# Attention and two gated layers on one core: TensorE's attention work grouped by kinds in half-unit steps

## The chip, the cores and the metric

The kernel is one program on one core of a Trainium2 chip. A core has five engines with queues of their own, each in order: TensorE (PE, with its weight loads shown apart as PEld), VectorE (DVE), ScalarE (ACT), GpSimd (POOL) and SyncE (SP, which here only starts transfers). They wait for one another by semaphores. Operands lie in SBUF, products of TensorE in the eight banks of PSUM. The metric is the time of one execution on the device in microseconds (us). The kernel before takes 571.85 us, the median of three runs (571.66 to 571.90).

## The reference

All in float32: causal attention (2 batches, 12 heads, 448 positions, 64 features a head), its output laid out as 896 tokens by 768 features, then two layers on those tokens.

```python
scores = scale * np.matmul(q, k.transpose(0, 1, 3, 2))      # (2, 12, 448, 448)
scores = np.where(mask, -1000000000.0, scores)              # causal
attn = np.exp(scores - np.max(scores, axis=-1, keepdims=True))
attn = attn / (np.sum(attn, axis=-1, keepdims=True) + 1e-09)
x = np.matmul(attn, v).transpose(0, 2, 1, 3).reshape(896, 768)
x = (x @ w_a) * (x @ w_b) @ w_out                           # 768 -> 1536 -> 768
h = x @ w_in                                                # 768 -> 2048
out = (h * (1.0 / (1.0 + np.exp(-h)))) @ w_out2             # 2048 -> 768
```

## The kernel before

**The layers.** Products are taken as three passes: an operand is split into a rounded half `hi` and a remainder `lo` (type float32r), and hi·hi + hi·lo + lo·hi is summed in a PSUM bank (`mm`, L295). ScalarE makes `hi` by a copy, VectorE makes `lo` by a subtraction. Weights arrive as raw words and go through conversion steps on ScalarE (L213, L219, L252) and VectorE (L225, L230, L256), laid out by `Timeline.convert` over a stretch of the program. A stretch is measured in matmuls that have been written so far; in the attention part a slot counts as seven (`SLOT_MM`). The weights of the first granule (a pair of weight tiles) are converted over slots 8 to 34, those of the second over slots 35 to 52. Later granules use products of sums of blocks, for which sums of the input chunks are needed (`sums_of`, in steps from slot 44).

**Attention.** A unit is two heads of one batch, 12 units in all, the first six of batch 0. Its 448 queries are seven chunks `j` of 64; chunk `j` sees keys 0 to 64(j+1). The chunks go in four groups, `GROUPS = ((6,), (5, 0), (4, 1), (3, 2))`, one group a slot, four slots a unit. The stages of one group are these.

- `scores` (TensorE): chunks with j of 3 or more by the three passes in float32r, 128 keys by 128 queries to an array of 128x128 (L565); chunks 0 to 2, and all of unit 0, in plain float32 on half the columns of the array (L569, 128x64).
- `soft`: VectorE scales, masks and takes the minimum of the negated scores (L577), ScalarE takes the exponential and its sum (L581).
- `normalize`: VectorE forms the reciprocals of the sums for two groups at once (L590, L591), GpSimd multiplies the seven pieces `p` by them (L594).
- `transposes` (TensorE, float32, 128x128, L610): four 128x128 blocks a slot, written to one PSUM bank. They are copied to `ptr` in SBUF one slot later (L710), that of chunk 4 by VectorE, the six others by ScalarE.
- `pv` (TensorE, float32, 128x64, L627): the product with the values, `xo`, over four blocks of keys in three slots.
- `finish` / `arrive`: when `xo` is whole, ScalarE copies it twice, to `xh` (rounded, L383) and to `xf` (as it is, L385); VectorE makes `xl` (L389).

The halves of the next unit's `q` and `k` are made by GpSimd (`halves_hi`, L538) in a unit's first slot and VectorE (`halves_lo`, L543) in its third. The order on the engines is the order in which the program is written: in slot `s` stand the scores of group `s`, the `pv` of group `s-11`, the transposes of group `s-5`, and then what was put off to that slot, sorted by a priority (0 `finish`, 1 copies of transposes, 2 `soft`), then reciprocals, sums and conversions. PSUM banks: three for scores, two for transposes (`ps_t`; while batch 0 is unfinished a third), two for `xo`. From slot 50 on, TensorE also does products of the first layer that need batch 0 only (`early_products`).

**The end.** Each output block is copied from PSUM by ScalarE and sent by SP's queue (L920, L921). The very last one is cut in two: ScalarE copies and sends one half, VectorE and SP's queue the other (L914 to L917).

The order is set by these lines (L22 to L28 and L699):

```python
PV = ((0,), (1,), (2, 3), ())
EVAC_DVE = (4,)
LAG_N = 1
LAG_T = 5
LAG_PV = 11
ORDER = (("scores", 0), ("pv", LAG_PV), ("transposes", LAG_T))
...
for what, lag in ORDER:
    u, i = divmod(s - lag, NS)
```

Of the kernel before, what the change touches and what calls it, by code (L numbers as in the profile page):

```python
# [18 lines left out]
P = 128  # L19
D = 64  # L20
GROUPS = ((6,), (5, 0), (4, 1), (3, 2))
PV = ((0,), (1,), (2, 3), ())  # L22
COL = {j: c for c, j in enumerate(j for g in GROUPS for j in g)}
EVAC_DVE = (4,)
LAG_N = 1
LAG_T = 5
LAG_PV = 11
ORDER = (("scores", 0), ("pv", LAG_PV), ("transposes", LAG_T))  # L28
# [6 lines left out]
SLOT_HI = 0  # L35
SLOT_LO = 2
# [26 lines left out]
def fused_kernel(ctx: ExitStack, tc: tile.TileContext, qk, v, w_ab, w_mid, w_in, w_out, out):  # L63
# [327 lines left out]
    def sums_of(c):  # L391


        a11, a12, a21, a22 = (XF.pop((2 * c + i, b)) for b in range(B) for i in range(2))
# [11 lines left out]
        s3 = add("S", a11, a21, ALU.subtract)  # L406
        yield 2
# [69 lines left out]
    with tc.manual_schedule():  # L477

        with ExitStack() as actx:
# [33 lines left out]
            U = [dict() for _ in range(NU)]  # L513
            late, now = {}, [0]
            n_slots = NU * len(GROUPS) + LAG_PV + 2
            NS = len(GROUPS)
# [4 lines left out]
            def load_qk(u):  # L521
# [5 lines left out]
                nc.sync.dma_start(out=t["k"], in_=qk[u, :, 1, :])  # L527
# [22 lines left out]
            def scores(u, i):  # L550

                t = U[u]
                if i == 0:
                    for n in ("sums", "nmax", "rcp"):
                        t[n] = st_p.tile([P, NJ], F32, tag=n, name=n)
                bank = ps_s.tile([P, 512], F32, tag="s", name="sc")
                sm = sm_p.tile([P, S], F32, tag="sm", name="sm")
                o = 0
                for j in GROUPS[i]:
                    K = D * (j + 1)  # L560
                    sc = bank[:, o:o + K]
                    o += K
                    if "qh" in t and j >= BIG:
                        for n, (a, k) in enumerate((("qh", "kh"), ("qh", "kl"), ("ql", "kh"))):
                            nc.tensor.matmul(out=sc, lhsT=t[a][:, j - BIG].rearrange("p h q -> p (h q)"), rhs=t[k][:, 0:K],  # L565
                                             start=(n == 0), stop=(n == 2))
# [6 lines left out]
                    defer(0, 2, partial(soft, u, j, sc, sm[:, o - K:o], K, COL[j]))  # L573
# [25 lines left out]
            def transposes(u, i):  # L599
                t = U[u]  # L600
                if i == 0:
                    t["pt"] = pt_p.tile([P, NKB, 2, S], F32, tag="ptr", name="ptr")
                pool, tag = (ps_g[1], "g") if now[0] < b0_done - 4 and now[0] % 3 == 0 else (ps_t, "t")
                bank = pool.tile([P, NKB, 2, D], F32, tag=tag, name="pt")
                o = 0
                for j in GROUPS[i]:
                    pt = bank[:, o:o + nblk[j]]
                    o += nblk[j]
                    for kb in range(nblk[j]):
                        nc.tensor.transpose(  # L610
                            out=pt[:, kb].rearrange("p h q -> p (h q)"),
                            in_=p_sb[u % 2][j][:, kb * P:(kb + 1) * P], identity=ident,
                        )
                    copy = nc.vector.tensor_copy if j in EVAC_DVE else nc.scalar.copy
                    dst = t["pt"][:, 0:nblk[j], :, j * D:(j + 1) * D]
                    defer(1, 1, partial(copy, out=dst, in_=pt))

            def pv(u, kb):
# [12 lines left out]
                if kb == NKB - 1:  # L631
                    defer(1, 0, partial(finish, b, chunk, t["x"][:, 0:S]))
# [29 lines left out]
            line.now = -n_slots * SLOT_MM  # L662
            line.convert(granules[0], (CONV0 - n_slots) * SLOT_MM, (CONV1 - CONV0) * SLOT_MM)
            line.convert(granules[1], (CONV1 + 1 - n_slots) * SLOT_MM, (CONV2 - CONV1) * SLOT_MM)
# [11 lines left out]

            b0_done = (NP - 1) * NS + LAG_PV + NKB + 1
            fill, n_fill = early_products(), 2 * NP
            done_fill = 0
            fill0 = NU * NS + 2  # L680
            for s in range(n_slots):
                now[0] = s
                if s == NU * NS + 1:
# [5 lines left out]
                u, i = divmod(s, NS)  # L689
                if i == 0 and 0 < u and u + 2 < NU:  # L690
                    load_qk(u + 2)
                if i == SLOT_HI and u + 1 < NU:
                    halves_hi(u + 1)
                if i == SLOT_LO and u + 1 < NU:
                    halves_lo(u + 1)
                if i == 0 and 0 < u <= NU:
                    load_v(u - 1)
                for what, lag in ORDER:
                    u, i = divmod(s - lag, NS)  # L699
                    if not 0 <= u < NU:  # L700
                        continue
                    if what == "scores":
                        scores(u, i)
                    elif what == "transposes":
                        transposes(u, i)
                    else:
                        for kb in PV[i]:
                            pv(u, kb)
                for _, fn in sorted(late.pop(s, ()), key=lambda e: e[0]):
# [3 lines left out]
                u, i = divmod(s - LAG_N, NS)  # L713
                if 0 <= u < NU and i % 2 == 1:
                    normalize(u, (i - 1, i))
                if s >= SUMS0:
                    sums_x.step()
                line.to((s + 1 - n_slots) * SLOT_MM)
# [257 lines left out]
```

## Time and profile before

| | |
|---|---|
| median of 3 runs | 571.85 us |
| the profiled execution: its time, its span | 571.69 us, 569.9 us |
| TensorE busy | 559.3 us (98%), clock 0.999 |
| VectorE busy | 421.8 us (74%) |
| ScalarE busy | 380.5 us (67%) |
| GpSimd busy | 72.2 us (13%), all of it before 97 us |
| chain that ended last | PE 93%, DVE 2%, ACT 2%, POOL 1%, issue 1%, DMA 1% |
| last attention product on TensorE | ends at about 107.4 us |

The attention part is the first 107 us of the span, the two layers are the rest, in which TensorE has no gap. Times in the rows further down count from the start of the span. A row of a timeline gives the start, the duration and the instruction; durations of neighbours on one engine overlap, since an engine starts the next instruction before the last has drained, so what an instruction takes of its engine is read from one start to the next. "[1.00 <-ACT ptr L710]" at a row's end means that the engine had been idle for 1.00 us and that the instruction at L710 on ACT, which writes `ptr`, let it go on.

### The profile page before, as it was taken

How to read it: one execution, taken by the hardware profiler on the slowest of the kernel's cores; microseconds unless marked ns; L12 is line 12 of the kernel's file. 1: busy time of each engine (PE TensorE's matmuls, PEld its weight loads, DVE VectorE, ACT ScalarE, POOL GpSimd, SP SyncE). 2: the span in 40 equal slices, each digit the busy share in tenths (PEclk: the TensorE clock that was granted, in tenths of full speed). 3: DMA queues.
4: the chain of work that ended last, by engine and by line, in shares of the span. 5: the costliest groups of instructions: out<-in, count | busy, mean ns of one | idle time of the engine just before them, and what ended most of it. 6: DMA issues, size and time to landing. Idle time of an engine off the chain costs nothing.

```text
span 569.9 us, 8400 instructions
## 1 busy us (share of the span) xinstructions
PE 559.3 (98%) x2978; PEld 490.4 (86%) x2978; DVE 421.8 (74%) x794; ACT 380.5 (67%) x754; POOL 72.2 (13%) x127
## 2 busy tenths in 40 slices
PE   8999997999999999999999999999999999999997
PEld 6666664799999999999999999999999999999996
DVE  6798887587989898969875688978887798342500
ACT  4989988674766666668745475888786996532601
POOL 6887764000000000000000000000000000000000
PEclk9999999999999999999999999999999999999999
DMA  7355323032333434333333333333324233541501
GB/s 246 116 178 139 121 65 141 1 112 110 112 110 112 136 134 161 117 118 109 114 110 112 110 112 110 112 113 110 112 96 143 75 113 111 165 142 54 176 0 64
DMA packets 18233, 65.41 MB, mean 115 GB/s; under 512 B 2192, under 2 KB 6928, under 8 KB 18192
## 3 DMA queue, kind: packets, MB, share of 16 engines
q1 hardware_dynamic: 18048, 64.77, 33.6%
q8 instruction: 23, 0.38, 0.3%
q14 instruction: 18, 0.15, 0.1%
q10 hardware_dynamic: 144, 0.11, 0.1%
HBM read 62.13 MB, written 2.75 MB: 114 GB/s over the span
## 4 chain that ended last, share of the span: by engine, by line
PE 93%; DVE 2%; ACT 2%; POOL 1%; issue 1%; DMA 1%; SPq 0%; POOLq 0%; DVEq 0%; ACTq 0%
PE acc L295 82%; PE pt L610 4%; PE xo L627 3%; PE sc L565 3%; PE sc L569 2%; DVE sm L577 1%; POOL p L594 1%; ACT ptr L710 1%; DMA k<-qk 1%; DVE wq L230 0%; ACT xf L385 0%; ACT p L581 0%; ACT xh L383 0%; DVE kl L543 0%; DVE ql L543 0%
## 5 line engine op out<-in xcount | busy, mean ns | idle before, releaser
L225 DVE SCALAR_TENSOR_TENSOR wq<-wr 128x768 uint32<-128x768 uint32 (+1 forms) x76 | 66.5, 877 | 28.4 <-ACT wr L219 27.7
L318 ACT COPY s<-acc 128x448 f32<-128x448 f32 x72 | 38.4, 533 | 63.1 <-PE acc L295 62.7
L219 ACT ACTIVATE wr<-wr,wbias 128x768 uint32<-128x768 uint32 (+1 forms) x76 | 69.9, 920 | 0.0
L213 ACT ACTIVATE wr<-wr 128x768 f32<-128x768 f32 (+1 forms) x76 | 63.8, 840 | 5.4 <-DMA wr<-w_out 4.0
L230 DVE SCALAR_TENSOR_TENSOR wq<-wr,wq 128x768 uint32<-128x768 uint32 (+1 forms) x76 | 64.0, 873 | 0.1
L594 POOL TENSOR_SCALAR p<-p,rcp 128x448 f32<-128x448 f32 (+6 forms) x84 | 56.3, 685 | 21.3 <-ACT p L581 15.6
L581 ACT ACTIVATE p<-sm,nmax 128x448 f32<-128x448 f32 (+6 forms) x84 | 43.0, 523 | 10.5 <-DVE nmax L577 9.5
L295 PE MATMUL acc<-th,wgbl 128*128 128x448 f32 x168 | 49.5, 366 | 0.0
L295 PE MATMUL acc<-th,wgbh 128*128 128x448 f32 x168 | 49.4, 366 | 0.0
L295 PE MATMUL acc<-th,wgal 128*128 128x448 f32 x168 | 49.4, 365 | 0.0
L295 PE MATMUL acc<-tl,wgah 128*128 128x448 f32 x168 | 49.4, 366 | 0.0
L295 PE MATMUL acc<-tl,wgbh 128*128 128x448 f32 x168 | 49.4, 365 | 0.0
L295 PE MATMUL acc<-th,wgah 128*128 128x448 f32 x168 | 49.3, 365 | 0.0
L610 PEld LDWEIGHTS pt<-ident,p 128*128 128x128 f32 x192 | 20.2, 141 | 22.4 <-issue 10.8
L610 PE MATMUL pt<-ident,p 128*128 128x128 f32 x192 | 31.0, 285 | 5.5 <-ACT ptr L710 4.4
L577 DVE CUSTOM_DVE_ANT_0 sm<-sc,mask 128x448 f32<-128x448 f32 (+6 forms) x84 | 31.9, 411 | 4.8 <-PE sc L569 4.8
L295 PEld LDWEIGHTS acc<-th,wgbh 128*128 128x128 f32 x168 | 31.5, 188 | 2.9 <-DVE s L767 0.2
L295 PEld LDWEIGHTS acc<-th,wgah 128*128 128x128 f32 x168 | 31.5, 188 | 2.7
L295 PEld LDWEIGHTS acc<-tl,wgah 128*128 128x128 f32 x168 | 31.6, 188 | 2.6
L295 PEld LDWEIGHTS acc<-th,wgal 128*128 128x128 f32 x168 | 31.5, 188 | 2.5
L295 PEld LDWEIGHTS acc<-th,wgbl 128*128 128x128 f32 x168 | 31.5, 188 | 2.5
L295 PEld LDWEIGHTS acc<-tl,wgbh 128*128 128x128 f32 x168 | 31.5, 188 | 2.5
(167 smaller groups left out, 1384.2 us busy)
## 6 DMA issues: line engine op xcount, KB each, us to landing
wr<-w_ab SPq DMA_DIRECT2D x24, 768.0 KB, 4.9
wr<-w_in SPq DMA_DIRECT2D x16, 768.0 KB, 4.5
wr<-w_out SPq DMA_DIRECT2D x24, 512.0 KB, 4.4
wr<-w_mid SPq DMA_DIRECT2D x12, 768.0 KB, 4.6
v<-v SPq DMA_DIRECT2D x12, 256.0 KB, 4.2
q<-qk SPq DMA_DIRECT2D x24, 112.0 KB, 2.8
k<-qk SPq DMA_DIRECT2D x12, 224.0 KB, 3.3
out<-o SPq DMA_DIRECT2D x11, 224.0 KB, 5.4
```

The source lines that it names most:

```text
L213: nc.scalar.activation(out=word(i, 1).bitcast(F32), in_=word(i, 1).bitcast(F32), func=AF.Copy, scale=2.0 ** -112)
L219: nc.scalar.activation(out=word(i, 0), in_=word(i, 0), func=AF.Relu, bias=wbias, scale=2.0 ** -29)
L225: nc.vector.scalar_tensor_tensor(out=xi(i), in0=word(i, 1), scalar=3, in1=word(i, 0), op0=ALU.logical_shift_left, op1=ALU.bitwise_or)
L230: nc.vector.scalar_tensor_tensor(out=xi(i), in0=word(i, 1), scalar=0x80000000, in1=xi(i), op0=ALU.bitwise_and, op1=ALU.bitwise_or)
L295: nc.tensor.matmul(out=acc[:, 0:S], lhsT=w, rhs=a, start=first, stop=last, skip_group_check=True)
L318: nc.scalar.copy(out=t, in_=acc[:, 0:S])
L565: nc.tensor.matmul(out=sc, lhsT=t[a][:, j - BIG].rearrange("p h q -> p (h q)"), rhs=t[k][:, 0:K], start=(n == 0), stop=(n == 2))
L577: nc.vector.tensor_tensor_reduce(out=sm, in0=sc, in1=mask[:, S - K:S], op0=ALU.add, op1=ALU.min, scale=-(D ** -0.5), scalar=3.0e38, accum_ ...
L581: nc.scalar.activation(out=p_sb[u % 2][j][:, 0:K], in_=sm, func=AF.Exp, bias=t["nmax"][:, c:c + 1], scale=-1.0, accum_out=t["sums"][:, c:c ...
L594: nc.gpsimd.tensor_scalar(out=pj, in0=pj, scalar1=t["rcp"][:, COL[j]:COL[j] + 1], scalar2=1.0, op0=ALU.mult, op1=ALU.mult,)
L610: nc.tensor.transpose(out=pt[:, kb].rearrange("p h q -> p (h q)"), in_=p_sb[u % 2][j][:, kb * P:(kb + 1) * P], identity=ident,)
L627: nc.tensor.matmul(out=t["x"][h * D:(h + 1) * D, kb * P:S], lhsT=t["v"][:, kb, h * D:(h + 1) * D], rhs=t["pt"][:, kb, h, kb * P:S], start= ...
```

## The change

The slot becomes a step of two groups, two steps a unit, and in a step TensorE's work is ordered by kinds: first the float32r scores of both groups, then the plain ones, then `pv` (key blocks 0 and 1 in one step, 2 and 3 in the other), then all eight transposes. The lags become `LAG_T = 2` and `LAG_PV = 5` steps. The eight transposed blocks go to two banks and leave by seven copies in a new split (`COPIES`): in the first step one by ScalarE and three by VectorE, in the second three by ScalarE. ScalarE's copies have priority 0 now, `finish` 1, `halves_lo` and `soft` 2, VectorE's copies and `normalize` 3. A third bank is used in turn for units 0 to 7.

`arrive` makes no `xf` for batch 0; `sums_of` makes that chunk anew from `xh` and `xl` by an addition on VectorE (`whole`). The keys of unit 0 are sent for by ScalarE's queue instead of SP's. The early products are spread over four steps and stand first in a step. The last output block is no longer cut in two.

```diff
+COPIES = (
+    ((0, "scalar", 0, 2, 5, 2), (1, "vector", 2, 1, 5, 2), (1, "vector", 3, 1, 6, 1), (1, "vector", 0, 1, 0, 1)),
+    ((0, "scalar", 0, 1, 1, 4), (1, "scalar", 1, 1, 2, 3), (1, "scalar", 2, 1, 4, 1)),
+)
+LAG_T = 2
+LAG_PV = 5
+FILL_STEPS = 4
...
-        XF[chunk, b] = t = A.new(F32, "xf")
-        nc.scalar.copy(out=t, in_=src)
+        if b:
+            XF[chunk, b] = t = A.new(F32, "xf")
+            nc.scalar.copy(out=t, in_=src)
...
+    def whole(chunk):
+        hi, lo = XS[chunk, 0]
+        t = A.new(F32, "xf")
+        nc.vector.tensor_tensor(out=t, in0=hi[:].bitcast(F32), in1=lo[:].bitcast(F32), op=ALU.add)
+        return t
...
-                nc.sync.dma_start(out=t["k"], in_=qk[u, :, 1, :])
+                (nc.sync if u else nc.scalar).dma_start(out=t["k"], in_=qk[u, :, 1, :])
...
+                if groups[0] and u + 1 < NU:
+                    defer(0, 2, partial(halves_lo, u + 1))
+                for n in range(len(groups)):
+                    defer(0, 2, partial(soft_group, u, [(j, sc) for m, j, sc in work if m == n]))
...
+                for _ in range(2):
+                    pool, tag = (ps_g[1], "g") if n_banks[0] % 3 == 2 and u < NP + 2 else (ps_t, "t")
...
+                    if copy == "vector":
+                        defer(1, 3, partial(nc.vector.tensor_copy, out=dst, in_=src))
+                    else:
+                        defer(1, 0, partial(nc.scalar.copy, out=dst, in_=src))
...
+                while done_fill < min(n_fill * max(0, d + 1 - 2 * NU) // FILL_STEPS, n_fill):
+                    next(fill, None)
+                    done_fill += 1
+                if u < NU:
+                    scores(u, (2 * i, 2 * i + 1))
+                u, i = divmod(d - LAG_PV, 2)
+                if 0 <= u < NU:
+                    for kb in range(2 * i, min(2 * i + 2, NKB)):
+                        pv(u, kb)
+                u, i = divmod(d - LAG_T, 2)
+                if 0 <= u < NU:
+                    transposes(u, i)
+                u, i = divmod(d - 1, 2)
+                if 0 <= u < NU:
+                    defer(0, 3, partial(normalize, u, (2 * i, 2 * i + 1)))
...
-                if last and b == 1 and i == 1:
-                    o2, half = A.new(F32, "o2"), S // 2
...
+                nc.scalar.copy(out=o, in_=src)
+                nc.sync.dma_start(out=out[m + i, :, toks[b]], in_=o)
```

TensorE, first half of a unit in the middle of attention, before. `sc` are scores, `xo` the product with the values, `pt` the transposed pieces.

```order
L565 MATMUL sc<-kh,qh 128x448
L565 MATMUL sc<-kl,qh 128x448
L565 MATMUL sc<-kh,ql 128x448
L627 MATMUL xo<-ptr,v 64x320 x2
L610 MATMUL pt<-ident,p_3_124 128x128 x2
L610 MATMUL pt<-ident,p_2_123 128x128 x2
L565 MATMUL sc<-kh,qh 128x384
L565 MATMUL sc<-kl,qh 128x384
L565 MATMUL sc<-kh,ql 128x384
L569 MATMUL sc<-k,q_119 64x64 x2
L627 MATMUL xo<-ptr,v 64x192 x2
L627 MATMUL xo<-ptr,v 64x64 x2
```

The same half of a unit on TensorE after the change.

```order
L581 MATMUL sc<-kh,qh 128x448
L581 MATMUL sc<-kl,qh 128x448
L581 MATMUL sc<-kh,ql 128x448
L581 MATMUL sc<-kh,qh 128x384
L581 MATMUL sc<-kl,qh 128x384
L581 MATMUL sc<-kh,ql 128x384
L585 MATMUL sc<-k,q_119 64x64 x2
L667 MATMUL xo<-ptr,v 64x192 x2
L667 MATMUL xo<-ptr,v 64x64 x2
L655 MATMUL pt<-ident,p_6_134 128x2x64 x3
L655 MATMUL pt<-ident,p_6_134 128x128
L655 MATMUL pt<-ident,p_5_133 128x2x64 x3
```

The two groups of float32r scores stand in one piece, behind them everything on half the array, behind that seven of the half's eight transposes (the eighth is the next row).

ScalarE around the arrival of one unit of batch 0, before. `xo` is the finished product, `ptr` the transposed pieces in SBUF, `p` the exponentials.

```order
L383 CAST xh<-xo 128x448
L385 COPY xf<-xo 128x448
L710 COPY ptr<-pt 128x8x64
L581 ACTIVATE p_4_132,sums<-sm,nmax 128x320
L581 ACTIVATE p_1_129,sums<-sm,nmax 128x128
L710 COPY ptr<-pt 128x6x64
L710 COPY ptr<-pt 128x2x64
L581 ACTIVATE p_3_131,sums<-sm,nmax 128x256
L581 ACTIVATE p_2_130,sums<-sm,nmax 128x192
L710 COPY ptr<-pt 128x2x64
```

And after the change, over the same exponentials.

```order
L750 COPY ptr<-pt 128x4x128
L383 CAST xh<-xo 128x448
L608 ACTIVATE p_4_132,sums<-sm,nmax 128x320
L608 ACTIVATE p_1_129,sums<-sm,nmax 128x128
L608 ACTIVATE p_3_131,sums<-sm,nmax 128x256
L608 ACTIVATE p_2_130,sums<-sm,nmax 128x192
L750 COPY ptr<-pt 128x2x256
L750 COPY ptr<-pt 128x2x192
L750 COPY ptr<-pt 128x2x64
```

The copy of transposes stands ahead of `xh`, there is no `xf`, and the copies of a half stand together instead of one behind each group.

VectorE where the last unit's scores are worked on, after the change. `xf<-xh,xl` is the new addition of `whole`, `S` the sums.

```order
L617 TENSOR_SCALAR sums<-sums 128x4
L618 RECIPROCAL rcp<-sums 128x4
L396 TENSOR_TENSOR xf<-xh,xl 128x448
L408 TENSOR_TENSOR S<-xf 128x448
L604 ISA sm,nmax<-sc,mask 128x320
L604 ISA nmax 128x1
L604 ISA sm,nmax<-sc,mask 128x128
L604 ISA nmax 128x1
L604 ISA sm,nmax<-sc,mask 128x256
L604 ISA nmax 128x1
L604 ISA sm,nmax<-sc,mask 128x192
L604 ISA nmax 128x1
```

The addition stands ahead of the last unit's `sm`; the sums' first subtraction stood in the same part of the program before, with `xf` read as ScalarE had left it.

## Rows read from the trace of the kernel before

**Rows 1.** Windows: us, then busy us (instructions) of PE, PEld, DVE, ACT, POOL; clock; DMA

```profile
27.37:63.70 36.33, 36.33 (x282) 24.33 (x280) 33.06 (x120) 33.85 (x116) 30.29 (x47) 1.00 0.47 144
27.37:41.90 14.53, 14.53 (x114) 9.73 (x112) 14.12 (x49) 12.91 (x47) 12.44 (x18) 1.00 0.46 157
73.50:85.00 11.50, 11.23 (x88) 7.59 (x89) 11.36 (x38) 8.97 (x34) 9.33 (x12) 1.00 0.25 74
```

**Rows 2.** Waits from 19 to 108 us: total us, times, longest

```profile
PE pt L610 <- ACT ptr L710: 4.4, 6, 1.4
DVE xl L389 <- ACT xf L385: 9.6, 7, 2.4
```

**Rows 3.** Timeline of TensorE: start us, us, tile<-operands, shape, count, [idle before <-releaser]

```profile
57.12 0.66 PE L610 MATMUL pt<-ident,p 128*128 128x128 f32 x4
57.53 0.45 PE L565 MATMUL sc<-kh,qh 128*128 128x448 f32 x1
57.82 0.36 PE L565 MATMUL sc<-kl,qh 128*128 128x448 f32 x1
58.02 0.37 PE L565 MATMUL sc<-kh,ql 128*128 128x448 f32 x1
58.31 0.76 PE L627 MATMUL xo<-ptr,v 128*64 128x320 f32 x4
...
61.85 0.44 PE L569 MATMUL sc<-k,q 128*64 128x128 f32 x4
62.22 0.66 PE L610 MATMUL pt<-ident,p 128*128 128x128 f32 x4
```

**Rows 4.** Timeline of TensorE, two transposes that wait

```profile
73.48 0.63 PE L610 MATMUL pt<-ident,p 128*128 128x128 f32 x4 [1.00 <-ACT ptr L710]
...
89.95 0.63 PE L610 MATMUL pt<-ident,p 128*128 128x128 f32 x4 [1.39 <-ACT ptr L710]
```

**Rows 5.** Timeline of ScalarE around one arrival

```profile
63.70 0.55 ACT L385 COPY xf<-xo 128x448 f32<-128x448 f32 x1
64.13 0.61 ACT L710 COPY ptr<-pt 128x512 f32<-128x512 f32 x1
64.61 0.59 ACT L581 ACTIVATE p<-sm,nmax 128x320 f32<-128x320 f32 x1
```

**Rows 6.** Timeline of VectorE

```profile
57.71 0.93 DVE L256 TENSOR_TENSOR wgbl<-wq,wgbh 128x768 fp32r<-128x768 f32 x1
...
82.77 1.09 DVE L230 SCALAR_TENSOR_TENSOR wq<-wr,wq 128x768 uint32<-128x768 uint32 x1
83.78 0.55 DVE L710 COPY ptr<-pt 128x384 f32<-128x384 f32 x1
84.25 0.61 DVE L577 CUSTOM_DVE_ANT_0 sm<-sc,mask 128x448 f32<-128x448 f32 x1
...
85.08 0.59 DVE L398 TENSOR_TENSOR S<-xf 128x448 f32<-128x448 f32 x1
```

**Rows 7.** Timeline of GpSimd, the same three scalings twice

```profile
43.75 1.49 POOL L594 TENSOR_SCALAR p<-p,rcp 128x448 f32<-128x448 f32 x3 [0.83 <-ACT p L581]
...
57.96 2.04 POOL L594 TENSOR_SCALAR p<-p,rcp 128x448 f32<-128x448 f32 x3 [0.84 <-ACT p L581]
```

**Rows 8.** Timeline of TensorE, the first scores

```profile
5.17 3.52 PE L569 MATMUL sc<-k,q 128*64 128x448 f32 x28 [0.34 <-DMA k<-qk]
```

**Rows 9.** The last output: timeline; lines L920, L921 (ns, us); L917

```profile
566.52 0.34 ACT L914 COPY o<-acc 128x224 f32<-128x224 f32 x1 [1.92 <-PE acc L295]
...
566.90 0.39 DVE L915 COPY o<-acc 128x224 f32<-128x224 f32 x1 [20.18 <-ACT o L914]
...
L920 ACT COPY o<-acc x11: 532/534/546, 487.0 to 564.1; 128x448 f32<-128x448 f32 x11
...
DMA to landing us min/median/max: 1.9/5.4/6.2
...
DMA to landing us min/median/max: 1.7/1.7/1.7
```

More of the change, by code (lines that the diff above doesn't have):

```diff
@@ L389, in arrive @@
         return lambda: nc.vector.tensor_tensor(out=lo, in0=src, in1=hi[:].bitcast(F32), op=ALU.subtract)
+    def whole(chunk):
[3 more added lines that the diff above has]
+        return t
     def sums_of(c):
-        a11, a12, a21, a22 = (XF.pop((2 * c + i, b)) for b in range(B) for i in range(2))
+        a21, a22 = (XF.pop((2 * c + i, 1)) for i in range(2))
+        a11, a12 = whole(2 * c), None
+        yield 1
         def add(name, a, b, op):
@@ L406, in sums_of @@
         s3 = add("S", a11, a21, ALU.subtract)
+        yield 1
+        a12 = whole(2 * c + 1)
         yield 2
@@ L661, in fused_kernel @@
             load_ahead()
[L662 to L664 removed]
+            line.now = -2 * n_steps * SLOT_MM
+            line.convert(granules[0], (CONV0 - 2 * n_steps) * SLOT_MM, (CONV1 - CONV0) * SLOT_MM)
+            line.convert(granules[1], (CONV1 + 1 - 2 * n_steps) * SLOT_MM, (CONV2 - CONV1) * SLOT_MM)
             first = []
@@ L675, in early_products @@
                         yield
[L677 to L683, printed above, removed]
+            fill, n_fill, done_fill = early_products(), 2 * NP, 0
+            for d in range(n_steps):
+                now[0] = d
+                u, i = divmod(d, 2)
+                if u == NU and i == 0:
                     sctx.close()
@@ L688, in fused_kernel @@
                     banks.add(ctx.enter_context(right(name="ps_r", bufs=3, space=PSUM, reuse_waits="tile")), 3)
-                u, i = divmod(s, NS)
                 if i == 0 and 0 < u and u + 2 < NU:
                     load_qk(u + 2)
-                if i == SLOT_HI and u + 1 < NU:
+                if i == 0 and u + 1 < NU:
                     halves_hi(u + 1)
-                if i == SLOT_LO and u + 1 < NU:
-                    halves_lo(u + 1)
                 if i == 0 and 0 < u <= NU:
                     load_v(u - 1)
[L698 to L709, printed above, removed]
+                while done_fill < min(n_fill * max(0, d + 1 - 2 * NU) // FILL_STEPS, n_fill):
[13 more added lines that the diff above has]
+                    defer(0, 3, partial(normalize, u, (2 * i, 2 * i + 1)))
+                for _, fn in sorted(late.pop(d, ()), key=lambda e: e[0]):
                     fn()
@@ L712, in fused_kernel @@
                     tasks.pop(0)()
[L713 to L718, printed above, removed]
-                want = n_fill * max(0, s + 1 - fill0) // (n_slots - 3 - fill0)
-                while done_fill < min(want, n_fill):
-                    next(fill, None)
-                    done_fill += 1
+                for n in range(2):
+                    if 2 * d + n >= SUMS0:
+                        sums_x.step()
+                    line.to((2 * d + n + 1 - 2 * n_steps) * SLOT_MM)
             run(fill)
```

85 lines of the change are left out of this document (41 added, 44 removed).

## The prediction

> **What bounds the kernel now.** I read the page first: TensorE is busy for 98% of the span at full clock, and the chain that ended last is 93% TensorE. Of the layers the change touches only the last output. So I read the attention part by windows. Five units between two starts of `xo` for keys of block 0 take 36.33 us, 7.27 us each, and TensorE is busy for all of it [rows 1]. The others are not far behind: per unit ScalarE is busy 33.85/5 = 6.77, VectorE 6.61, GpSimd 6.06 us. In two of these units VectorE has 14.12 of 14.53 us, and from 73.50 to 85.00 us 11.36 of 11.50 [rows 1]. The reader is to see that TensorE sets the pace with little air behind it. Next I asked who lets TensorE go on: in the attention part it waits 4.4 us in six places, each time before transposes, until ScalarE has emptied a bank [rows 2, 4]. Last I read one unit on TensorE start by start, for what a change of kind costs.
>
> **TensorE's work by kinds.** The three float32r passes over 448 columns start at 57.53, 57.82 and 58.02, and the next kind at 58.31: 0.29, 0.20 and 0.29 us for equal work [rows 3]. The middle one has its own kind on both sides, so entering a group of this kind costs 0.09 and leaving it 0.09. A unit has four such groups before and two after: 4 x 0.09 = 0.36 saved. In all a unit goes from 14 changes of kind to 8. The other two that go are entries into transposes. 64-query scores with 128 columns take 0.37 from their start to the transposes [rows 3]; how much of it is the change no row shows alone. From below it is 0; from above 0.17, if such a change costs what entering and leaving a float32r group do together. I take 0.14, near the upper end, since four small matmuls lie in those 0.37. So 0.36 + 2 x 0.14 = 0.64 a unit (bounds 0.36 and 0.70): 6.63 in place of 7.27. From the first `xo` to the last scores nine units are done: 9 x 0.64 = 5.8 us (3.2 to 6.3). Behind the last scores the order has about nine changes fewer, at 0.1 each 0.9 us (0.4 to 1.4).
>
> One rule of the Trainium skill speaks against the full term. TensorEngine Tiling, section Key Properties, says that changing the tiling mode drains the engine, and that changing the tile within a mode doesn't. By it only the changes between 128x128 and 128x64 cost anything, eight a unit before and four after. The row agrees at 58.31, where 128x64 follows; it differs at 57.53, where the array stays 128x128 behind transposes and the first pass is still 0.09 slower [rows 3].
>
> **What waits for ScalarE.** For batch 0 `xf` goes: 0.43 us from start to start, in six units [rows 5]. Transposes leave by four copies in place of six, 1536 columns in place of 1664; at 0.48 us for 512 columns [rows 5] that is 0.12 a unit at least, and with two starts less I take 0.2. ScalarE's 6.77 becomes 6.14 a unit, inside the 6.63. The copies now stand ahead of `xh` instead of behind `xh` and `xf`, which is some 0.8 us of queue before the copy that TensorE waits for. Of the 4.4 us [rows 2] I let 2.4 go (bounds 0 and 4.4): the conversion steps in ScalarE's queue stay where they were, and with them part of waits as long as 1.00 and 1.39 [rows 4].
>
> **What VectorE gets.** Three copies of 512 columns in all in place of one of 384, which takes 0.47 from start to start [rows 6]: 128 columns more are 0.16, two more starts 0 to 0.3; I take 0.3 a unit. Where conversions fall (1.01 each from start to start [rows 6]) there is no room. The two units to 41.90 need 14.12 + 0.6 = 14.7 us of VectorE against 2 x 6.63 = 13.3 of TensorE: 1.5 over, of which I let 0.3 be absorbed, +1.2. From 73.50 to 85.00 us TensorE's 11.23 busy us [rows 1] are 1.54 units and become 10.2, VectorE's 11.36 becomes 11.8: +1.6. In those late units only two banks serve the transposes, and the second transposes of a unit wait for VectorE's copies, which stand behind `ql`, `kl` and four `sm`; three places at up to 0.6, mostly the same waits, +0.3. The early products come first in the step behind the last scores and write where scores were, so they wait for VectorE's last `sm`: 0 to 1.0, I take +0.3. New waits: +3.4 (bounds 0, if short queues hide them all, and 6.5).
>
> The six additions of `whole` take about 0.5 each, as the like subtraction `S` [rows 6]. Two stand near the last scores, four behind, where VectorE had air: it stood idle for `xf` up to 2.4 us at once, 9.6 in all [rows 2], and `xh` alone comes sooner. I cost them at nothing on the path; without that cover they cost 3.0. GpSimd's three scalings take 1.49 us beside copies from PSUM and 2.04 beside a conversion that reads two tiles of SBUF [rows 6, 7]. The Trainium skill, SBUF — State Buffer, section SBUF: two separate sides, gives the reason: such an instruction and GpSimd lock each other out of a shared port pair for its whole length. By that rule two additions ahead of the last scalings would hold TensorE up by up to 1.0 more, 566.7.
>
> **Start and end.** TensorE waits 0.34 us for the first keys [rows 8]. Sent for by a queue that is free, they land behind the warm-up products: -0.3 (0 to -0.34). What queues behind that issue on ScalarE is its table load, far ahead of its first exponential. SP's next loads start one issue earlier. At the end, before, VectorE's half starts at 566.90, only when ScalarE's is done; its 0.39 us and 1.7 to landing [rows 9] end at 569.0. After, one copy of 0.53 starts at 566.52 like ScalarE's half before, and its transfer takes at least 1.9 [rows 9]: 569.0 as well. I cost it at 0 (-0.3 to +0.5; the median of 5.4 was measured with weights in flight, of which none are left).
>
> **The sum.** -5.8 - 0.9 - 2.4 + 3.4 - 0.3 + 0 = -6.0 us. The profiled execution took 571.69 us (569.9 of span and 1.8 around it), 0.16 under the median of 571.85. 571.69 - 6.0 = 565.7 us. All bounds together give from -13 to +3 us.
>
> **The rivals.**
>
> *VectorE becomes the bound all through.* For: 6.61 + 0.3 = 6.91 a unit, above TensorE's 6.63, and two windows without air [rows 1]. Against: the 6.61 holds two of the most loaded units, and VectorE now finds `xh` ready, where it waited 9.6 us [rows 2]. At 97% use a unit takes 7.12: 9 x 0.15 = 1.3 gained, with 0.9 and 0.8 of the other terms 568.7.
>
> *Slower: the shorter way from sums to transposes.* Five slots, 9.1 us, become two steps, 6.6 us. In between stand VectorE's whole next step, with the reciprocals last in it, and three scalings of 1.5 to 2.0 [rows 7]. I count 0.5 to 1.0 us of air: VectorE's reciprocals 2.2 to 3.9 us into a step, the scalings, then the transposes 5.3 to 6.2 us after that step's start. A VectorE that lags by 2 us stalls every transpose of the step. It decides from 0.32 us of stall a step on, where the 0.64 a unit is used up; at 0.5 in 18 steps it costs 9 against 5.8 + 0.9 + 0.3 gained, with nothing else counted: 573.7. Against: a stalled TensorE has already given VectorE the step's scores, so the lag does not feed itself.
>
> *Only the drain counts* (the rule of the Trainium skill above). Four changes fewer a unit at about 0.11 are 0.46, 4.1 in nine units in place of 5.8: 567.4.
>
> *The waits vanish.* Copies first and no `xf` clear 4.0 of the 4.4, and VectorE's peaks are absorbed down to 1.2: -5.8 - 0.9 - 4.0 + 1.2 - 0.3, 561.9.
>
> **How the numbers follow.** The forecast of 565.7 has 0.50, the drain 0.12, VectorE as the bound 0.16, the slower case 0.12, vanishing waits 0.10. The range from 562.0 to 571.0 leaves out the lower part of the last (0.05) and the slower case with a little of the VectorE case (0.13). A measurement tells 0.2%, 1.1 us, from no change. Faster by more has the forecast, the drain, the last case and most of the VectorE case: 0.80. Within it: 0.09, from the VectorE and the slower case. Slower: 0.11.
>
> **What would show it.** Right: between two starts of `xo` for 448 columns some 6.6 us in the units that see no conversions, six float32r passes in a row with only the first and last at their longer spacing, TensorE's waits for `ptr` at about 2 us, and new waits of about 3 us for VectorE or GpSimd near the conversions. Wrong: a unit still above 7 us with TensorE waiting for `p` before most transposes (the way is too short), VectorE with no idle in all windows (it is the bound), or passes that each keep 0.29 (kinds cost nothing).

## The result, and the profile after

The changed kernel takes 566.94 us, the median of four runs (566.02, 566.10, 567.79, 568.01), against 571.88 of the kernel before in the same comparison: ratio 0.9914, 95% interval [0.9891, 0.9938]. 565.7 was forecast. The four runs fall into two pairs 1.8 us apart, and the rows below tell why. The profiled execution is of the upper pair: 568.01 us, span 566.2.

First the pace. Three units between two starts of `xo` for 448 columns, on the same view as [rows 1]:

```profile
42.87:62.86 19.99, 19.99 (x172) 15.40 (x168) 19.50 (x75) 18.14 (x60) 17.21 (x28) 1.00 0.53 166
```

19.99/3 = 6.66 us a unit in place of 7.27, TensorE again busy throughout, and VectorE is at 19.50 of 19.99 where it had 33.06 of 36.33. Inside a unit, beside [rows 3]:

```profile
57.59 1.09 PE L655 MATMUL pt<-ident,p 128*128 128x128 f32 x8
58.44 0.45 PE L581 MATMUL sc<-kh,qh 128*128 128x448 f32 x1
58.73 0.37 PE L581 MATMUL sc<-kl,qh 128*128 128x448 f32 x1
58.94 0.36 PE L581 MATMUL sc<-kh,ql 128*128 128x448 f32 x1
...
59.30 0.34 PE L581 MATMUL sc<-kl,qh 128*128 128x384 f32 x1
59.48 0.34 PE L581 MATMUL sc<-kh,ql 128*128 128x384 f32 x1
59.75 0.34 PE L585 MATMUL sc<-k,q 128*64 128x64 f32 x4
```

Of the six passes only the first (0.29 to the next start) and the last (0.27, where its like takes 0.18) are longer. Eight transposes take 58.44 - 57.59 = 0.85 us where nothing holds them up. TensorE's waits from 19 to 108 us, beside [rows 2]:

```profile
PE pt L655 <- DVE sums L617: 2.6, 2, 2.0
PE pt L655 <- ACT ptr L750: 0.7, 2, 0.4
PE pt L655 <- POOL qh L551: 0.4, 1, 0.4
PE pt L655 <- POOL p L621: 0.4, 1, 0.4
```

TensorE's waits for ScalarE fall from 4.4 to 0.7 us, and 3.4 us of new waits stand there instead, 2.6 of them for VectorE. (The list counts idle gaps alone; the section on why the prediction came out as it did reads the losses from start to start, where they are larger.) The largest wait, on TensorE:

```profile
79.19 0.33 PE L655 MATMUL pt<-ident,p 128*128 128x128 f32 x1
81.52 1.69 PE L655 MATMUL pt<-ident,p 128*128 128x128 f32 x7 [2.00 <-DVE sums L617]
82.86 0.72 PE L581 MATMUL sc<-kh,qh 128*128 128x448 f32 x1
83.38 0.57 PE L581 MATMUL sc<-kl,qh 128*128 128x448 f32 x1
83.75 0.57 PE L581 MATMUL sc<-kh,ql 128*128 128x448 f32 x1
...
90.53 0.95 PE L655 MATMUL pt<-ident,p 128*128 128x128 f32 x7 [0.55 <-DVE sums L617]
```

VectorE at that time:

```profile
77.93 0.94 DVE L556 TENSOR_TENSOR ql<-q,qh 128x512 fp32r<-128x512 f32 x1
78.79 0.61 DVE L556 TENSOR_TENSOR kl<-k,kh 128x448 fp32r<-128x448 f32 x1
79.33 0.48 DVE L604 CUSTOM_DVE_ANT_0 sm<-sc,mask 128x320 f32<-128x320 f32 x1
...
80.57 0.81 DVE L750 COPY ptr<-pt 128x256 f32<-128x256 f32 x3
81.30 0.15 DVE L617 TENSOR_SCALAR sums<-sums 128x3 f32<-128x3 f32 x1
```

The list of waits names `sums`, the instruction that ended last before 81.52; what the transposes wait for is the copies just ahead of it, which empty the bank. These copies had their data from about 76.5 on, when the transposes of the step before had ended, and stood behind `ql`, `kl` and four `sm`. What follows is dearer than it looks: the passes for 448 columns are now 0.52, 0.37 and 0.37 from start to start, 0.29, 0.21 and 0.19 in the unit above. The granted clock of that stretch:

```profile
79.20:81.50 2.30, 0.32 (x3) 0.13 (x2) 2.27 (x14) 1.59 (x7) 1.21 (x3) 1.00 0.86 307
81.50:85.10 3.60, 3.58 (x13) 3.14 (x13) 2.40 (x5) 1.52 (x6) 2.19 (x3) 0.53 0.29 49
```

It is 0.53 there, near its lower level of 1.2 GHz, and full on both sides. What is missing of full speed over 3.6 us, 0.47 x 3.6 = 1.7, is nearly the distance between the pairs of runs; the run of 567.79 has a mean clock of 0.997 like the profiled one, that of 566.02 has 1.000.

At the start the keys come in time: the first scores begin at 4.76 without a wait, in place of 5.17 [rows 8]. But the first two sets of transposes wait for GpSimd:

```profile
4.76 4.14 PE L585 MATMUL sc<-k,q 128*64 128x448 f32 x28
...
11.66 1.22 PE L655 MATMUL pt<-ident,p 128*128 128x128 f32 x8 [0.61 <-POOL p L621]
...
15.03 1.64 PE L655 MATMUL pt<-ident,p 128*128 128x128 f32 x8 [0.65 <-POOL p L621]
...
20.59 0.92 PE L667 MATMUL xo<-ptr,v 128*64 128x448 f32 x4
```

The first `xo` starts at 20.59; before it started at 19.88. The end, beside [rows 9], has one copy, and one transfer behind it:

```profile
562.91 0.53 ACT L946 COPY o<-acc 128x448 f32<-128x448 f32 x1 [1.92 <-PE acc L295]
```

From that copy to the end of the span it is 566.2 - 562.9 = 3.3 us; before it was 569.9 - 566.5 = 3.4.

### The profile page after: what moved, and what is told of

Its sections match the earlier page's. It is cut to its first block, busy times and chain, and to the rows that moved or that the text cites. A ratio compares the mean times of both kernels' runs of the same rounds, so it can differ in the third digit from the quotient of the medians.

```text
span 566.2 us, 8377 instructions
## 1 busy us (share of the span) xinstructions
PE 556.0 (98%) x2978; PEld 495.2 (87%) x2978; DVE 429.3 (76%) x823; ACT 375.2 (66%) x724; POOL 72.6 (13%) x127
## 4 chain that ended last, share of the span: by engine, by line
PE 89%; DVE 5%; POOL 2%; issue 2%; ACT 1%; DVEq 0%; ACTq 0%; POOLq 0%
PE acc L295 82%; PE pt L655 2%; DVE sm L604 2%; PE sc L581 2%; POOL p L621 2%; PE xo L667 1%; PE sc L585 1%; PE wp L687 1%; DVE ptr L750 1%; DVE kl L556 1%; DVE sums L617 0%; ACT p L608 0%; POOL qh L551 0%; DVE wgal L256 0%; DVE wgbl L256 0%
## 5 line engine op out<-in xcount | busy, mean ns | idle before, releaser
L608 ACT ACTIVATE p<-sm,nmax 128x448 f32<-128x448 f32 (+6 forms) x84 | 41.8, 503 | 15.5 <-DVE nmax L604 15.4
```

The costliest lines, as they stand in the source:

```text
L608: nc.scalar.activation(out=p_sb[u % 2][j][:, 0:K], in_=sm, func=AF.Exp, bias=t["nmax"][:, c:c + 1], scale=-1.0, accum_out=t["sums"][:, c:c ...
```

## The experiments

Theory: TensorE sets the pace and its changes of kind are what the change takes off; VectorE's copies behind its own queue, with two banks, give part of it back, and the fallen clock gives back more in some executions. Rivals: the gain comes from fewer copies and no `xf` on ScalarE; the new order itself (the short way) makes the waits; the difference between the runs is something else than the clock.

### e1_bank3: a third bank for all units

```diff
-                    pool, tag = (ps_g[1], "g") if n_banks[0] % 3 == 2 and u < NP + 2 else (ps_t, "t")
+                    pool, tag = (ps_g[1], "g") if n_banks[0] % 3 == 2 else (ps_t, "t")
```

> Third bank for the transposes in all units instead of the first eight. Theory (the long wait of TensorE near 79.5 us comes from having two banks, behind VectorE's copies, and the half clock after it comes from that wait): the 2.0 us wait shrinks to 1 us or less, bounded by GpSimd's scalings which end near 80.4, no stretch at clock 0.5 between 75 and 90 us in any run, so all runs lie together at 564.5 to 566.0 and none near 568. Rival (VectorE is simply late there, banks are not what holds): the wait stays at about 2 us, released by something else, runs still fall in two clusters 1.8 us apart, median 566 to 568.

563.89 us (563.65 to 564.58), ratio to before 0.9863 [0.9851, 0.9876], clock 1.000 in all four runs. The wait of 2.0 us is gone. In the same step the eight transposes now stand in one row, 1.45 us from their start to the next scores:

```profile
78.05 1.69 PE L655 MATMUL pt<-ident,p 128*128 128x128 f32 x8
79.50 0.45 PE L581 MATMUL sc<-kh,qh 128*128 128x448 f32 x1
```

What is left is a wait of 0.45 for GpSimd in the step behind it, at 82.61.

The changed kernel's wait of 0.4 that its list puts down to `qh` is gone here too, so it was a bank's as well. The two banks cost 2.2 us even at full clock (566.06, the mean of the lower pair, to 563.89) and 4.0 where the clock falls. This is the lowest median of all versions, though no better than e10_both beyond the noise.

### e2_xf: `xf` of batch 0 by ScalarE again

```diff
-        if b:
-            XF[chunk, b] = t = A.new(F32, "xf")
-            nc.scalar.copy(out=t, in_=src)
+        XF[chunk, b] = t = A.new(F32, "xf")
+        nc.scalar.copy(out=t, in_=src)
...
-        hi, lo = XS[chunk, 0]
...
+        return XF.pop((chunk, 0))
```

> ScalarE copies xf for batch 0 again and the six additions on VectorE go; all else as in the change. Theory (this part is worth little on the path: ScalarE has air in the units of batch 0, VectorE gets air at the end): within 1 us of the change's 566.9, with less VectorE work between 86 and 92 us. Rival 1 (freeing ScalarE is what let the rest gain): 2 us or more slower than the change, 569 or more, with new waits for ptr copies. Rival 2 (the additions cost their full 3 us on VectorE): 564 or less.

567.87 us (566.77 to 569.33, six runs), ratio 0.9932 [0.9916, 0.9948]. Three runs have the fallen clock (0.997: 568.25, 569.26, 569.33), three have not (566.77, 566.82, 567.50); at full clock, three runs against two, it is about 0.8 us above the changed kernel's 566.06. TensorE's waits for ScalarE are 1.5 us in place of 0.7, the same 0.8 more. The part is worth some 0.8, not the bulk. The run shows the balance alone: the additions on VectorE cost less than the copies on ScalarE that they replace.

### e3_split: the second group's float32r scores behind the first group's other work

Only TensorE's order changes; a half has two float32r groups again, with work on half the array between them.

```diff
-                for n, j, sc in sorted(work, key=lambda e: e[1] < BIG):
+                for n, j, sc in work:
+                    if n and work[0][0] == 0 and between:
+                        between.pop(0)()
...
+                between = [partial(pv, w, kb) for kb in range(2 * h, min(2 * h + 2, NKB))] if 0 <= w < NU else []
```

> TensorE's order alone: in each step the second group's float32r scores stand behind the first group's plain scores and the first product with the values, so four float32r groups a unit again, transposes still in one piece. Other engines keep their order. Theory (a change of kind costs TensorE about 0.09 on entering and 0.09 on leaving a float32r group): a unit without other waits takes 6.67 + 0.36 = 7.03 us (6.95 to 7.15), in the whole 1.5 to 4 us slower than the change, since units that wait for other engines lose less. Rival (kinds cost nothing, the gain came from earlier copies and less ScalarE work): a unit stays at 6.67, total within 0.5 us of the change.

570.99 us (570.82 to 573.47, twelve runs), ratio 0.9993 [0.9984, 1.0003]: nearly the whole gain is gone. (The two runs above 573 have a clock of 0.994.) Two units on its TensorE:

```profile
50.35:65.07 14.72, 14.72 (x117) 9.77 (x115) 13.28 (x51) 11.65 (x39) 11.45 (x19) 1.00 0.33 99
```

7.36 a unit against 6.66. VectorE now has air, 13.28 of 14.72. The four changes of tile shape (128x128 to 128x64 or back) that came back cost 0.70/4 = 0.17 each, about twice what I had expected of them.

### e4_ends: first keys by SP, last output in halves, as before

```diff
-                (nc.sync if u else nc.scalar).dma_start(out=t["k"], in_=qk[u, :, 1, :])
+                nc.sync.dma_start(out=t["k"], in_=qk[u, :, 1, :])
...
+                if last and b == 1 and i == 1:
+                    o2, half = A.new(F32, "o2"), S // 2
```

> Both ends as before the change: the first keys on SyncE's queue, the last output in two halves; the middle as in the change. Read from the profile. Theory (the last output is worth nothing; the early keys are worth 0.3 us at the first scores but the start is bounded later by GpSimd's scalings): the first scores start 0.3 to 0.4 us later than in the change (near 5.2), the first product with the values starts within 0.3 us of the change's 20.6, and the last landing comes 2.4 to 2.7 us after the last matmul as in the change. Rival (the ends matter): 0.3 us or more at either end carried to the total.

One run: 566.03 us, as the changed kernel's lower pair. The wait for the keys is back, and the first `xo` starts no later (20.10):

```profile
5.06 3.34 PE L585 MATMUL sc<-k,q 128*64 128x448 f32 x28 [0.23 <-DMA k<-qk]
```

With the last copy at 560.87 and the span at 564.2, the end takes 3.3 us in halves too. Neither end of the change is worth anything that this one run shows. Its wait for VectorE at 81.01 was also 2.00 long, but the clock stayed full.

### e5_warm: TensorE kept busy in the wait

Eight products of a zero tile, into a bank that nothing reads, ahead of the transposes that wait. (A plain float32 product stands as two records in the rows, so the eight are x16.)

```diff
+                if d == 21:
+                    wq = ps_g[1].tile([P, 512], F32, tag="g", name="wp")
+                    for _ in range(8):
+                        nc.tensor.matmul(out=wq[:, 0:P], lhsT=wz, rhs=wz, start=True, stop=True)
```

> Eight matmuls of zeros written to an unused bank stand where TensorE waits 2.0 us in step 21; nothing is taken away. Theory (the two clusters of times, 566.0 and 567.9, differ by whether the clock falls to half after that wait): the wait is filled, the clock stays at 1.0, all runs near 566.0 (565.7 to 566.5), none near 567.9. Rival (the clusters have another cause): runs at both values as before, or all later by the 1.7 us of the added matmuls.

566.14 us (565.88 to 566.45), ratio 0.9901 [0.9888, 0.9914], the clock full in the profiled run. The transposes start when they did, and the passes behind them keep 0.28 and 0.20:

```profile
79.14 2.05 PE L747 MATMUL wp<-wz 128*128 128x128 f32 x16
...
81.48 0.95 PE L655 MATMUL pt<-ident,p 128*128 128x128 f32 x7 [0.18 <-DVE sums L617]
82.19 0.45 PE L581 MATMUL sc<-kh,qh 128*128 128x448 f32 x1
82.47 0.36 PE L581 MATMUL sc<-kl,qh 128*128 128x448 f32 x1
```

None of the four runs is near 568. The wait itself is still there, filled with work of no use, and the times are those of the lower pair. At one fallen run in two, four full ones would come by chance once in sixteen times; with the spacing of the passes behind the wait, 0.52 in one trace and 0.28 in the other, the 1.8 us between the pairs are put down to the clock. Of the profiled runs, this one and that of the changed kernel start their first `xo` at like times (20.56 and 20.59) and end 568.01 - 566.45 = 1.6 apart.

### e6_lag3: transposes and `pv` one step later (on e1_bank3)

```diff
-LAG_T = 2
-LAG_PV = 5
+LAG_T = 3
+LAG_PV = 6
```

> On top of the third bank for all units, transposes stand three steps behind the scores instead of two and the product with the values six instead of five, so the program is one step longer. Theory (what is left of waiting, some 4 us between 20 and 90 us, comes from the short way from the sums over GpSimd's scalings to the transposes): units that took 7.4 to 7.9 us come down towards 6.7, TensorE's waits for GpSimd nearly vanish, 1 to 3 us faster than with the third bank alone (561 to 563), less what the longer end gives back. Rival (VectorE's full stretches set the pace there, not the way): the same units stay at 7.4 or more and the total is within 0.7 us of 563.9 or above it.

565.44 us (565.17 to 567.03), ratio 0.9894 [0.9877, 0.9912]: 1.5 slower than e1_bank3. Eight units from the first `xo` take 79.72 - 24.12 = 55.6 us against 76.66 - 20.04 = 56.6, so the longer way saves about 1.0 of waits in the middle. It is paid for at the start, where the first `xo` comes 4.1 us later; from the ninth `xo` to the end 1.5 come back (563.4 - 79.72 = 483.7 against 561.9 - 76.66 = 485.2). At the start the clock falls too, behind a wait of 1.68:

```profile
17.86 0.98 PE L655 MATMUL pt<-ident,p 128*128 128x128 f32 x7 [1.68 <-ACT ptr L750]
...
19.18 0.42 PE L581 MATMUL sc<-kh,qh 128*128 128x256 f32 x1
19.39 0.42 PE L581 MATMUL sc<-kl,qh 128*128 128x256 f32 x1
```

The passes for 256 columns are 0.21 apart, 0.11 to 0.12 in stretches at full clock. Here the fall shows no price in the total: this run of 565.17 is the fastest of the four, the one whose clock stayed at 1.000 took 565.51.

### e7_whole and e7_halves: two more changes of kind, the shape kept

Both on e6_lag3, in a step that begins with the plain scores and `pv`, so that transposes stand next to the float32r scores. In the first all transposes come ahead of both float32r groups, in the second half of them between the two. Of the edits, the scores of e7_whole against the changed kernel, and the two lines that e7_halves adds to e7_whole:

```diff
+                large = [w for w in work if "qh" in t and w[1] >= BIG]
...
+                for m in range(2):
+                    for n, j, sc in large:
+                        if n == m:
+                            product(j, sc)
+                    yield
...
                 tr = transposes(u, i) if 0 <= u < NU else iter(())
+                next(tr, None)
+                next(sc, None)
                 run(tr)
                 run(sc)
```

> Control for the next run, on top of the third bank and the longer lags: in a step TensorE does plain scores, products with the values, all eight transposes, then the float32r scores of both groups. The same eight changes of kind and four of tile shape a unit as in the change. Both theories: 6.65 to 6.75 us a unit where nothing waits.

> As the control, but the second half of the transposes stands between the two groups of float32r scores. Two more changes of kind a step, none of tile shape (all is 128x128). Theory 1 (every change of kind costs): +0.18 us a step, a unit 6.95 to 7.1. Theory 2, the skill's rule (only a change of tiling mode drains the array): a unit stays within 0.08 us of the control's.

600.01 us, ratio 1.0495 [1.0476, 1.0515], and 596.75, ratio 1.0444 [1.0417, 1.0471]. As totals they tell nothing of kinds: this order makes transposes wait for ScalarE in most steps (23.7 us in the first). The spacing inside a step can be read all the same. e7_whole, then e7_halves:

```profile
51.00 0.98 PE L665 MATMUL pt<-ident,p 128*128 128x128 f32 x7 [1.69 <-ACT ptr L762]
51.74 0.45 PE L581 MATMUL sc<-kh,qh 128*128 128x448 f32 x1
...
53.06 0.64 PE L585 MATMUL sc<-k,q 128*64 128x128 f32 x6
```

```profile
50.68 0.55 PE L665 MATMUL pt<-ident,p 128*128 128x128 f32 x3 [1.76 <-ACT ptr L764]
50.98 0.45 PE L581 MATMUL sc<-kh,qh 128*128 128x448 f32 x1
...
51.66 0.60 PE L665 MATMUL pt<-ident,p 128*128 128x128 f32 x4
52.02 0.42 PE L581 MATMUL sc<-kh,qh 128*128 128x384 f32 x1
...
52.72 0.76 PE L585 MATMUL sc<-k,q 128*64 128x128 f32 x8
```

Seven transposes and six passes take 53.06 - 51.00 = 2.06 us in one piece and 52.72 - 50.68 = 2.04 cut in two, at full clock; one unit earlier it is 2.06 and 2.05. The two more changes between float32 transposes and float32r scores, both on 128x128, cost nothing that shows.

### e8_finish_first: `finish` ahead of ScalarE's copies (on e1_bank3)

```diff
-                        defer(1, 0, partial(nc.scalar.copy, out=dst, in_=src))
+                        defer(1, 1, partial(nc.scalar.copy, out=dst, in_=src))
...
-                    defer(1, 1, partial(finish, b, chunk, t["x"][:, 0:S]))
+                    defer(1, 0, partial(finish, b, chunk, t["x"][:, 0:S]))
```

> The kernel with the third bank for all units (563.9 us), with finish and ScalarE's copies of transposes in the order of the kernel before: finish at priority 0, the copies at 1, so xh (and xf for batch 1) stands ahead of the copy of each unit. If the place of the copies is what took ScalarE's waits away, transposes wait again for ScalarE's ptr once a unit, some 0.4 us (0.43 for xh in batch 0, 0.86 for xh and xf in batch 1): 2 to 4 us of such waits against 0.9 with the copies first, and the time goes to about 566. If instead four copies in place of six and the missing xf did it, nothing changes: 563.6 to 564.5.

565.13 us (564.79 to 565.73), ratio 0.9884 [0.9870, 0.9899], 1.2 us above e1_bank3: its fastest run lies above the slowest of e1_bank3 (564.58), though the intervals of the two ratios just overlap (0.9870 and 0.9876). TensorE's waits for ScalarE, e8_finish_first and then e1_bank3:

```profile
PE pt L655 <- ACT ptr L750: 2.0, 3, 1.3
```

```profile
PE pt L655 <- ACT ptr L750: 0.9, 2, 0.4
```

1.1 more of waits and 1.2 more of time: the place of the copies is worth about that much, between what the two theories said. The rest of the 4.4 us of waits stays away. No run isolates what took it; `xf` is 0.8 of it (e2_xf), and fewer copies, the coarser steps and, in this run, the third bank are left for the rest.

### e9_dve_first: VectorE's copies ahead of `soft` (two banks as in the changed kernel)

```diff
-                        defer(1, 3, partial(nc.vector.tensor_copy, out=dst, in_=src))
+                        defer(1, 1, partial(nc.vector.tensor_copy, out=dst, in_=src))
```

> The changed kernel (two banks from unit 8 on), with VectorE's three copies of transposes at priority 1, ahead of halves_lo and soft, in place of 3. If the wait of 2.0 us of step 21 is the queue that stands ahead of these copies on VectorE, it goes, the granted clock stays full, and the time is 564 to 565 in every run; VectorE's soft comes up to 1 us later in the step, which costs nothing if the air in GpSimd's way suffices. If that air doesn't suffice, transposes wait for p (GpSimd) instead, 0.3 us and more in most steps, and the time is 568 or above.

564.46 us (564.27 to 564.85), ratio 0.9870 [0.9854, 0.9887]. In the same step:

```profile
79.04 0.88 PE L655 MATMUL pt<-ident,p 128*128 128x128 f32 x6
80.19 0.44 PE L655 MATMUL pt<-ident,p 128*128 128x128 f32 x2 [0.27 <-POOL p L621]
```

The wait takes both, the queue ahead of the copies and a bank that has to be emptied first: with the copies at the head of VectorE's queue two banks do nearly as well as three, and with three banks (e1_bank3) the same queue makes no such wait.

### e10_both: third bank and VectorE's copies first

The two lines of e1_bank3 and e9_dve_first together.

> Third bank for all units (563.89 alone) and VectorE's copies ahead of soft (564.46 alone). If both edits only take the one wait of 2.0 us of step 21 away, together they give no more than the better one: 563.6 to 564.5. If the copies' place also shortens other waits, which the bank leaves at 1.7 us (0.9 for ScalarE, 0.8 for GpSimd), the time falls by up to 1.0: 562.9 to 563.5.

564.20 us (563.96 to 564.44), ratio 0.9868 [0.9852, 0.9885]: no faster than e1_bank3. Both edits take the same wait away.

## Why the prediction came out as it did

The frame held: TensorE sets the pace, its order carries the gain, and new waits give part of it back. The median lies 1.2 us above the forecast. Which changes of kind cost, and what makes the new waits, the prediction had wrong, so the nearness is partly luck. By its own terms:

- **Kinds, -5.8.** The size is right, 0.61 a unit for 0.64, and e3_split shows that it carries the change. The split is wrong. I gave each edge of a float32r group 0.09 and an entry into transposes 0.14. e7_halves against e7_whole shows changes within 128x128 free, so the 0.09 after transposes at 57.53 [rows 3] is not a price: what the first pass takes longer, the transposes before it take less (there 0.30 + 0.36 from start to start for three and four, 0.74 for seven in one piece). What is paid is the change between 128x128 and 128x64, eight a unit before and four after: 0.61/4 = 0.15 each, 0.17 by e3_split. That is the rule of the Trainium skill, TensorEngine Tiling, Key Properties, and these rows agree with it. So the mechanism that held is that of the rival *Only the drain counts*, at a higher price than the 0.11 I gave it; the forecast came to nearly the same size by counting changes that are free and paying too little for the others.
- **ScalarE's waits, -2.4: 3.7 went.** Undersized. The conversion steps that I let keep part of the waits stood in the queue as before, but only 0.7 of listed waits is left. The place of the copies is 1.2 of it (e8_finish_first, with the third bank), the missing `xf` some 0.8 (e2_xf).
- **VectorE, +3.4: more came, and in part by another way.** The list of waits has 3.4 of new ones, but it counts idle gaps, and a stall between two transposes hides in their rows. From start to start of `xo` the eight units from 20.59 on take 7.61, 6.74, 7.93, 6.66, 6.67, 6.66, 7.41 and 7.53 us: 57.2, which is 3.9 over eight at the pace of 19.99/3. Before, they took 60.0 (19.88 to 79.87), 1.9 over eight at 36.33/5.

  The first full stretch has the size that I gave it. Two units took 14.67 us, with VectorE busy for 14.53 (14.7 worked out); that is 1.3 over two at 6.66, for +1.2. But a lack of VectorE's time is not the whole of it: with one more step between scores and transposes (e6_lag3) the two units there take 13.37, TensorE without a gap and VectorE busy for 13.23. The changed kernel first, then e6_lag3:

```profile
28.20:42.87 14.67, 14.18 (x115) 10.24 (x112) 14.53 (x52) 11.16 (x39) 12.00 (x18) 1.00 0.40 131
36.33 1.78 PE L655 MATMUL pt<-ident,p 128*128 128x128 f32 x8
```

```profile
30.80:44.17 13.37, 13.37 (x116) 10.19 (x116) 13.23 (x52) 10.43 (x37) 11.68 (x19) 1.00 0.63 205
```

  The short way shows in the second row: these eight transposes take 1.53 us to the next scores at 37.86 in place of 0.85, until GpSimd's scalings end at 37.61 (3.31 us for four, shown at the end of this document).

  In the second stretch, for which I took 1.6, and 0.3 for its two banks, stand the waits of 2.00 and 0.55, from the very queue that the prediction names. "Three places at up to 0.6" is the step that failed: I bounded the wait by the lengths of single instructions and not by the sum of the queue ahead of the copies, 77.93 to 81.30. With a third bank VectorE works off the same queue and 2.2 us are saved. In the units from 20.59 and from 62.86 on it is ScalarE that is busy without a gap (7.61 of 7.61 us, and 14.94 of 14.94 for two units), so part of the 3.9 may be its own; no run separates that. The early products' 0.3 did not come.
- **The clock, not forecast.** +1.8 us between the pairs of runs, in two of four, from that wait; 1.6 between the two profiled runs that start alike.
- **Start, -0.3: +0.7 in the profiled execution**, +0.2 in those of e1_bank3 and e4_ends. The keys did come earlier, by 0.4. But the shorter way has no slack while the first unit fills it, and transposes wait 0.61 and 0.65 for the first scalings. I weighed that way as a rival for every step and not at the fill, where it bites first. The rest of the difference between executions lies in the first scores, 4.07 us in that of the changed kernel and 3.50 in e1_bank3. Their first two pairs of records, equal products over 448 columns, take 0.80 and 0.75 us from start to start in the former, 0.75 and 0.37 in e1_bank3: TensorE came up to full clock later. (The trace's record of the full clock begins at 6.5 and at 5.5 us.) In e4_ends, where it begins at 5.1, the scores start at 5.06 and take 3.27, and are done at 8.33, as early as those that started at 4.77 in e1_bank3 and ended at 8.27. So keys that came 0.3 earlier were worth nearly nothing, as the products began at the lower clock.
- **End, 0: 0.**

Together, from start to start in the profiled executions: +0.7 to the first `xo`; 57.2 us in place of 60.0 for the eight units behind it, -2.8 (4.8 gained by the pace, less 3.9 lost where 1.9 was lost before); 488.4 in place of 490.0 from there to the end, -1.6. That is -3.7, as measured (568.01 - 571.69). The last part holds the bank's wait and the fallen clock; in e1_bank3, without them, it takes 485.2. The 0.9 for changes of kind behind the last scores no run isolates. So the sum was near by errors that offset: ScalarE's waits gave back more than forecast, the new waits cost more, the start cost where a gain was forecast, and the clock was not thought of.

Of the rivals, VectorE as the bound all through fell: no idle, but 6.50 of busy time fitted into 6.66. The short way fell as a cost in every step, as three units run at 6.66 without a stall; it does cost at the fill and in the unit at 34.94, and e6_lag3 shows that about 1.0 of it is to be had in eight units, for 4.1 at the start. The 1.0 by which two additions might hold up the last scalings did not come either: the four scalings at 87.22, beside the first addition and the first subtraction, took 2.28 in all, no longer than elsewhere, and TensorE has no wait for them.

## What to carry to other kernels

Count TensorE's changes of tile shape, here 0.15 to 0.17 us each, before its changes of type or operation, and group by shape where TensorE is the bound. When a bank is emptied by an engine that has other work, the wait is the sum of what is queued ahead of the copy: put the copy first or give it another bank; here one of the two was enough. Read losses from start to start of one instruction that recurs, and not from a list of waits alone, which named 1.5 of 3.9 us here. Before trusting a gain of one per cent, look at the granted clock in the windows behind the longest new wait.

## What the runs showed of the hardware

- **TensorE's clock fell to its lower level behind waits of 2.00 and 1.68 us.** The granted clock was 0.53 from 81.50 to 85.10 after a wait of 2.00, and 0.51 from 19.00 to 22.50 in e6_lag3 after one of 1.68. It did not fall after 2.00 in e4_ends, nor after 1.89 in the profiled run of e3_split, nor before the change after 1.39 [rows 4]; which executions are hit is open. In the changed kernel TensorE was doing its usual work, nearly without a gap, up to the wait.
- **The change between 128x128 and 128x64 costs 0.15 to 0.17 us each**, the change between float32 transposes and float32r scores at 128x128 nothing that the rows can show (2.04 against 2.06).
- **GpSimd beside VectorE.** The four scalings of `p` for a second half took 2.28 us at 87.22, 3.31 at 34.30 when VectorE was doing `ql` and `kl`, and 3.94 when it was doing two conversion steps, `ql` and `kl`. The one over 128 columns took 0.37 beside VectorE's `sm` and 0.73 beside the subtraction `S`, which itself took 0.84 where its like took 0.59 [rows 6]:

```profile
34.30 3.31 POOL L621 TENSOR_SCALAR p<-p,rcp 128x320 f32<-128x320 f32 x4
...
43.63 0.37 POOL L621 TENSOR_SCALAR p<-p,rcp 128x128 f32<-128x128 f32 x1
...
76.47 3.94 POOL L621 TENSOR_SCALAR p<-p,rcp 128x320 f32<-128x320 f32 x4 [0.41 <-DVE rcp L618]
...
87.92 0.73 POOL L621 TENSOR_SCALAR p<-p,rcp 128x128 f32<-128x128 f32 x1
```

The Trainium skill, SBUF — State Buffer, section SBUF: two separate sides, has a VectorE instruction with two inputs in SBUF and a GpSimd instruction that reads SBUF lock each other out. These rows agree with it, the subtraction's included.
